# One transfer of q in five parts, with a matrix in its transposes that restores the order

## The chip, the cores and the metric

The kernel runs on one core of a Trainium2 chip. The metric is the device time of one execution in microseconds (us); smaller is better. The core has a matrix engine (TensorE, PE in the profile; its weight loads are PEld), VectorE (DVE), ScalarE (ACT), GpSimd (POOL) and SyncE (SP). Loads and stores are carried out by 16 DMA engines. POOL issues every load but one; SP issues that one and all stores.

## The reference

Two operators follow each other. The first is causal attention with a window of 64 positions, over 8 batches, 8 heads, 576 positions and a head dimension of 64:

```python
scores = scale * np.matmul(q, k.transpose(0, 1, 3, 2))
mask = (rel >= 0) & (rel < window)
scores = np.where(mask, scores, -1000000000.0)
attn = exp(scores - max); attn = attn / sum(attn)
return np.matmul(attn, v)
```

The second takes the result as x of shape 8 x 576 x 512, transforms it along the positions, multiplies the 64 lowest frequencies by one complex 512 x 512 matrix each (`w_r`, `w_i`), transforms back to y, forms u = x + y and returns u + max(u @ w_ch, 0). The 127 matrices that are needed (the imaginary one of frequency 0 has no effect) are 512 x 512 float32, 1 MiB each, and are by far the largest part of what is read from memory.

## The kernel before, in words

**Loads.** POOL issues a load for each of q, k and v of a batch (`load`, L109 to L112) and for each weight matrix (`load_w`, L138, one matrix; `load_two`, L144, two). The memory holds float32, the tiles in SBUF are bfloat16, and the transfer converts. A batch of q, 8 heads by 576 positions by 64, goes into a tile `rq` of 128 partitions x 2 x 1152: a partition's row in each of the two halves is a run of 18 positions of one head, 1152 elements, 4608 bytes in memory and 2304 in the tile. Half 0 holds heads 0 to 3 and half 1 heads 4 to 7, 32 partitions a head, in the order of the positions. A weight matrix goes into 128 partitions of 2048 elements. All loads go into one queue and are worked off in order.

**Order of the issues.** The first batches are loaded at the start. From then on `refill` (L402 to L414), called after each unit of transposes, loads batch b + 2 when a unit of batch b has freed its buffer, and one weight matrix behind it. The load of the last batch's q (b + 2 = 7) is issued after the q transposes of batch 5. Each issue on POOL waits in program order, for its buffer to be free and for the transfer that stands eight places before it to have landed, since the framework hands out eight completion semaphores in turn.

**Attention.** `transpose_units` (L234) gives 12 units a batch. Three `part`s each for k, v and q transpose 6 runs of 64 columns in two halves: the data tile is loaded as weights, and the identity `ident_bf` (128 x 128) is streamed through it, so that PSUM receives the transposed block; `evac` then copies it to `kT`, `vT` or `qT` with the columns in the order of positions. The column order that PSUM receives follows the matrix that is streamed. Scores, exponentials and the weighted sums follow in windows of 512 columns (`scores`, L305; `weigh`, L332), the transform of a finished batch in `dft` (L361).

**Weights.** From about 141 us on, `half(i)` (L610) multiplies matrix i: 16 matmuls per matrix, in the order of `order`, which is the order of the loads. When a matrix has been used, `issue` (L567) loads the next one into its place. Between the matrices PE does the second product, the inverse transform (L748 to L843), and, where there is nothing else, filler matmuls (`idle`, L901).

**End.** The last matrix is used by `half(T_I + 1)` (L1006). Behind it stand the last products, the rectification and the stores (L1008 to L1055), which can't start before it.

The order on PE and POOL is that of the program inside `manual_schedule`; on DVE and ACT the framework orders instructions in the main loop.

Of the kernel before, what the change touches and what calls it, by code (L numbers as in the profile page):

```python
# [11 lines left out]
BF16 = mybir.dt.bfloat16  # L12
# [8 lines left out]
def view(ap, off, dims):  # L21

    return bass.AP(ap.tensor, ap.offset + off, [list(ap.ap[0])] + [list(d) for d in dims])
# [3 lines left out]
def kernel(  # L27
# [10 lines left out]
    nc = tc.nc  # L38
    B, H, S, D = q.shape
# [8 lines left out]
    RUN = S // 32  # L48
# [6 lines left out]
    def evac(o, i, on_act):  # L55

        if on_act:
            return nc.scalar.copy(out=o, in_=i)  # L58
        return nc.vector.tensor_copy(out=o, in_=i)  # L59
# [10 lines left out]
    ident_bf = consts.tile([128, 128], BF16, name="ident_bf")  # L70
# [19 lines left out]
    acons = p1.enter_context(tc.tile_pool(name="acons", bufs=1, side="right"))  # L90
# [10 lines left out]
    RAW = {"k": k, "q": q, "v": v}  # L101

    def raw_tile(which):
        return rawp.tile([128, 2, RUN * D], BF16, name="r" + which)

    def runs(b, which):
        return RAW[which][b].rearrange("(x g) (p c) d -> (g p) x (c d)", g=4, c=RUN)

    def load(b, which):  # L109
        r = raw_tile(which)  # L110
        nc.gpsimd.dma_start(out=r, in_=runs(b, which))
        raws[b, which] = r  # L112


# [63 lines left out]
    with tc.manual_schedule(engines=ALL_FOUR):  # L178
# [3 lines left out]
        with tc.tile_pool(name="tmpf", bufs=1, side="right") as tmp:  # L182
            mo = tmp.tile([128, NM], FP32, name="mo")
            to = tmp.tile([128, NT], FP32, name="to")
            nc.gpsimd.iota(mo, pattern=[[1, NM]], base=0, channel_multiplier=0,
                           allow_small_or_imprecise_dtypes=True)
            nc.gpsimd.iota(to, pattern=[[128, NT]], base=0, channel_multiplier=1,
                           allow_small_or_imprecise_dtypes=True)
            nc.gpsimd.memset(ident, 0.0)
            nc.gpsimd.affine_select(out=ident, in_=ident, compare_op=ALU.not_equal, fill=1.0,  # L190
                                    base=0, pattern=[[-1, 128]], channel_multiplier=1)
            load(0, "q")
            load(0, "v")
            for t0, t1 in ((0, 3), (3, NT)):
                n = t1 - t0
                mt = tmp.tile([128, 2, n * NM], FP32, name="mtf")
                nc.vector.tensor_tensor(out=view(mt, 0, [[NM, n], [1, NM]]), in0=view(mo, 0, [[0, n], [1, NM]]),
                                        in1=view(to, t0, [[1, n], [0, NM]]), op=ALU.mult)
                gen_trig(tmp, mt, n * NM, trigF[:, t0:t1, 0:NM], trigF[:, t0:t1, NM:2 * NM], "f")
                if t0 == 0:  # L200
                    nc.vector.tensor_copy(out=ident_bf, in_=ident)
        nc.scalar.activation(out=spark, in_=ident[:, 0:1], func=ACT_F.Exp)
        raws[0, "k"] = raw_tile("k")
        for c, engine in enumerate((nc.vector, nc.gpsimd, nc.vector)):
            cc = slice(6 * D * c, 6 * D * (c + 1))
            engine.tensor_copy(out=raws[0, "k"][:, :, cc], in_=k_first[:, :, cc])
        load(1, "k")
        for i in range(4):
            half = i % 2
# [24 lines left out]
    def transpose_units(b):  # L234

        rk, rq, rv = (raws.pop((b, which)) for which in "kqv")
        qT = qtp.tile([128, 4, S], BF16, name="qT")
        vT = vtp.tile([128, 4, S], BF16, name="vT")
        kT, vt = kTs[b % 2], vts[b % 2]
        qTs[b] = qT  # L240

        def part(src, dst, c0, on_act):
            def f():
                ps = ps_misc.tile([128, 6, 128], BF16, name="pst", tag="misc")
                for c in range(6):
                    for hh in range(2):
                        nc.tensor.transpose(out=ps[64 * hh:64 * hh + 64, c, :],  # L247
                                            in_=src[:, hh, (c0 + c) * D:(c0 + c + 1) * D],
                                            identity=ident_bf)
                evac(view(dst, c0, [[S, 4], [RUN, 32], [1, 6]]),  # L250
                     view(ps, 0, [[32, 4], [1, 32], [128, 6]]), on_act)
            return f

        def vback(u):
            def f():
                ps = ps_misc.tile([128, 6, 128], BF16, name="psv", tag="misc")
                for i in range(6):
                    a, j = divmod(6 * u + i, 9)
                    if j == 4:
                        parts = [(0, 64, 2 * a, 512), (64, 64, 2 * a + 1, 0)]  # L260
                    else:
                        parts = [(0, 128, 2 * a + (j > 4), 128 * j - (j > 4) * S)]
                    for r0, n, g, t0 in parts:
                        nc.tensor.transpose(out=ps[r0:r0 + n, i, :],  # L264
                                            in_=vT[:, g, t0:t0 + n], identity=ident_bf)
                evac(view(vt, 6 * u * VW, [[18 * VW, 2], [VW, 6], [1, D]]),
                     view(ps, 0, [[D, 2], [128, 6], [1, D]]), u != 1)
                if u:
                    hs = slice(u - 1, u + 2, 2)
                    nc.vector.tensor_copy(out=vt[64:128, 1, hs, 1:9], in_=vt[64:128, 0, hs, 0:8])  # L270
                    nc.vector.tensor_copy(out=vt[0:64, 1, hs], in_=vt[0:64, 0, hs])
            return f

        return [part(rk, kT, 0, True), part(rk, kT, 6, False), part(rk, kT, 12, True),
                part(rv, vT, 0, False), part(rv, vT, 6, True), part(rv, vT, 12, False),
                part(rq, qT, 0, True), part(rq, qT, 6, False), part(rq, qT, 12, True),
                vback(0), vback(1), vback(2)]

    def head_of(n):
# [143 lines left out]
    with tc.manual_schedule(engines=ALL_FOUR):  # L423
        first = transpose_units(0)
        for j in (0, 1, 2, 6, 7, 8):
            first[j]()
            refill(0, j)
            if j in (2, 8):
                warm_up(3)
        for half in range(2):  # L430
            pp = slice(64 * half, 64 * half + 64)
            nc.vector.tensor_copy(out=band2[pp], in_=band[pp, half, :])
        mask(0, 1)
        scores(0)
        for j in (3, 4, 5):
            first[j]()
            refill(0, j)
            warm_up(2)
        for vt in vts:
            nc.vector.memset(vt[:, 0, :, :, 64:66], 1.0)  # L440
        for j in (9, 10, 11):
            first[j]()
            refill(0, j)
        nc.vector.memset(pso, 1.0)
        nc.vector.tensor_copy(out=ident_r, in_=ident)
    with tc.manual_schedule(engines={E.PE, E.Pool}):
# [9 lines left out]
        def unit(b, j):  # L456
            if b not in units:
                units[b] = transpose_units(b)
            units[b][j]()
            refill(b, j)  # L460
            turned(b, j)

        for w in range(NWIN + 1):
# [22 lines left out]
            if w in (NWIN - 4, NWIN - 1):  # L486
                i = (B - 2) % 2 if w == NWIN - 4 else (B - 1) % 2
                spare(kTs[i])
                spare(qtp.tile([128, 4, S], BF16, name="qT"))
            if w in (NWIN - 4, NWIN):  # L490
                i = (B - 2) % 2 if w == NWIN - 4 else (B - 1) % 2
# [386 lines left out]
    for k, (f, delta, n, few) in enumerate(items):  # L878
        i = S_I + k * (T_I - 2 - S_I) // len(items)
# [25 lines left out]
    with tc.manual_schedule(engines=ALL_FOUR):  # L905
# [92 lines left out]
        for k in range(6):  # L998
# [10 lines left out]
                              in_=view(psys[0], 0, [[2 * B, NC], [2, B], [1, 2]]))  # L1009
# [78 lines left out]
```

## Time and profile before

| | us |
|---|---|
| median of three runs | 425.67 (425.48 to 425.93) |
| the profiled execution, its own time | 425.65 |
| its span, first to last instruction | 423.8 |
| PE busy | 352.3 |
| DVE, ACT, POOL busy | 189.2, 159.8, 81.6 |

The span of the profile is 1.85 us shorter than that execution's own time. In the profile's views a time is in us from the start of the span. In the view of windows, each engine has its busy time and the number of its instructions in the stretch, and the last two columns are the mean busy share of the 16 DMA engines and the GB/s that arrive (bytes in SBUF's types, half of what is read). The packets of one DMA engine overlap a little in the records, so a fully used set of 16 shows 1.04 to 1.10. In the timeline, what stands in brackets is the time that the engine stood idle before the row, and what ended it.

### The profile page before, as it was taken

The numbers are of one execution on the slowest core, as the hardware profiler recorded it, in microseconds if no ns is written. First come the engines' busy times: TensorE is split into PE (matmuls) and PEld (weight loads), VectorE is DVE, ScalarE is ACT, GpSimd is POOL, SyncE is SP. The second block draws the span as 40 slices with busy tenths as digits, with TensorE's granted clock in tenths as the row PEclk, the third lists the DMA queues.
The fourth block names the chain that finished last, engine by engine and source line by source line (L and its number), as shares of the span: only waits on it lengthen the run. The fifth ranks groups of instructions, "written<-read, shape, count | busy, mean of one in ns | idle before, by whom it ended". The sixth has DMA issues, their size and how long they took to land.

```text
span 423.8 us, 11438 instructions
## 1 busy us (share of the span) xinstructions
PE 352.3 (83%) x5156; PEld 233.6 (55%) x5185; DVE 189.2 (45%) x359; ACT 159.8 (38%) x267; POOL 81.6 (19%) x146
## 2 busy tenths in 40 slices
PE   7799999999997779866669587767789899998994
PEld 3466656656654567644446455545556565554451
DVE  6676775766764001634332351121104345340895
ACT  5565766767754100122102110110023343330863
POOL 6322222221031130411112012120121112200000
PEclk9999999999999555966756656666579999999997
DMA  8999999999999999999999999999999999995598
GB/s 212 211 214 212 214 212 212 213 213 213 214 214 214 213 215 261 215 214 214 215 214 213 215 213 215 215 213 215 213 215 214 214 213 211 214 214 106 203 370 320
DMA packets 29920, 92.55 MB, mean 218 GB/s; under 512 B 2352, under 2 KB 2352, under 8 KB 29872
## 3 DMA queue, kind: packets, MB, share of 16 engines
q0 software_dynamic: 24624, 81.21, 95.9%
q1 hardware_dynamic: 5248, 10.62, 6.8%
q8 instruction: 40, 0.66, 0.6%
q14 instruction: 8, 0.07, 0.0%
HBM read 162.53 MB, written 9.44 MB: 406 GB/s over the span
## 4 chain that ended last, share of the span: by engine, by line
PE 42%; DMA 39%; DVE 7%; issue 5%; ACT 3%; POOL 0%; DVEq 0%; POOLq 0%; ACTq 0%
DMA wms<-in_moe_w_r_dram 20%; DMA wms<-in_moe_w_i_dram 19%; PE psy L618 7%; PE pso L343 6%; PE pst L247 5%; PE psv L264 3%; PE psx L365 3%; PE pss L963 3%; DVE x_sb L351 2%; PE pss L956 2%; PE pss L300 2%; PE pss L319 2%; PE psy L903 2%; DVE vT L59 2%; PE psf L800 1%
## 5 line engine op out<-in xcount | busy, mean ns | idle before, releaser
L759 PE MATMUL psz<-wch,xT 128*128 128x512 f32 x144 | 65.0, 594 | 0.0
L753 DVE CAST xT<-pxt 128x1024 fp32r<-128x1024 bf16 x18 | 22.0, 1224 | 78.0 <-PE pxt L748 78.0
L762 ACT CAST Z<-psz 128x1024 fp32r<-128x1024 f32 x18 | 18.2, 1012 | 102.2 <-PE psz L759 94.5
L325 ACT ACTIVATE et<-pss 128x512 bf16<-128x512 f32 x72 | 39.2, 599 | 13.7 <-PE pss L319 13.7
L618 PE MATMUL psy<-XQ,wls 128*128 128x16 bf16 x560 | 22.0, 192 | 23.7 <-DMA wls<-in_moe_w_r_dram 14.2
L759 PEld LDWEIGHTS psz<-wch,xT 128*128 128x128 f32 x144 | 37.4, 287 | 5.9
L618 PE MATMUL psy<-XQ,wms 128*128 128x16 bf16 x624 | 25.1, 192 | 17.9 <-DMA wms<-in_moe_w_i_dram 12.7
L618 PEld LDWEIGHTS <-wls 128*128 128x128 bf16 x560 | 19.5, 106 | 33.8 <-DMA wls<-in_moe_w_r_dram 17.4
L618 PEld LDWEIGHTS <-wms 128*128 128x128 bf16 x624 | 21.4, 103 | 30.2 <-DMA wms<-in_moe_w_i_dram 15.3
L343 PE MATMUL pso<-vt,et 128*64 128x65 bf16 (+1 forms) x576 | 32.3, 203 | 3.5 <-DVE x_sb L351 1.6
L811 DVE TENSOR_TENSOR Z<-pse,Z 128x1024 fp32r<-128x1024 f32 x16 | 19.6, 1225 | 29.3 <-PE pse L800 29.3
L343 PEld LDWEIGHTS <-et 128*64 128x64 bf16 (+1 forms) x576 | 22.2, 109 | 14.2 <-issue 6.7
L351 DVE TENSOR_TENSOR x_sb<-pso,rcp 128x640 bf16<-128x640 f32 x32 | 26.3, 822 | 0.9
L618 PE MATMUL psy<-XQ,wt 128*128 128x16 bf16 x560 | 20.5, 192 | 4.8 <-DMA wt<-in_moe_w_i_dram 2.3
L618 PEld LDWEIGHTS <-wt 128*128 128x128 bf16 x560 | 18.3, 104 | 11.2 <-DMA wt<-in_moe_w_i_dram 4.3
L59 DVE CAST YT<-psy 128x256 fp32r<-128x256 f32 x6 | 2.5, 424 | 42.0 <-PE psy L618 32.7
L59 DVE COPY vT<-pst 128x768 bf16<-128x768 bf16 x16 | 15.3, 958 | 12.9 <-PE pst L247 11.3
L981 ACT ACTIVATE pss<-pss 128x512 f32<-128x512 f32 x35 | 18.5, 581 | 4.7 <-PE pss L963 4.1
L300 PE MATMUL pss<-band,ident_bf 64*64 64x512 bf16 x120 | 16.5, 396 | 0.0
L264 PE MATMUL psv<-ident_bf,vT 128*128 128x128 bf16 (+1 forms) x160 | 15.6, 226 | 0.6 <-DVE vT L59 0.6
L58 ACT COPY vt<-psv 128x768 bf16<-128x768 bf16 x16 | 12.9, 807 | 8.3 <-PE psv L264 8.2
L58 ACT COPY qT<-pst 128x768 bf16<-128x768 bf16 x16 | 12.9, 813 | 6.4 <-PE pst L247 6.4
(191 smaller groups left out, 605.7 us busy)
## 6 DMA issues: line engine op xcount, KB each, us to landing
wt<-in_moe_w_i_dram POOLq DMA_DIRECT2D x19, 512.0 KB, 20.4
wt<-in_moe_w_r_dram POOLq DMA_DIRECT2D x16, 512.0 KB, 19.4
wls<-in_moe_w_r_dram POOLq DMA_DIRECT2D x8, 1024.0 KB, 21.8
wms<-in_moe_w_i_dram POOLq DMA_DIRECT2D x7, 1024.0 KB, 22.2
wms<-in_moe_w_r_dram POOLq DMA_DIRECT2D x7, 1024.0 KB, 21.6
wls<-in_moe_w_i_dram POOLq DMA_DIRECT2D x6, 1024.0 KB, 21.3
rq<-in_q_dram POOLq DMA_DIRECT2D x8, 576.0 KB, 15.3
rv<-in_v_dram POOLq DMA_DIRECT2D x8, 576.0 KB, 13.8
```

What stands on the lines that cost most here:

```text
L58: return nc.scalar.copy(out=o, in_=i)
L59: return nc.vector.tensor_copy(out=o, in_=i)
L247: nc.tensor.transpose(out=ps[64 * hh:64 * hh + 64, c, :], in_=src[:, hh, (c0 + c) * D:(c0 + c + 1) * D], identity=ident_bf)
L264: nc.tensor.transpose(out=ps[r0:r0 + n, i, :], in_=vT[:, g, t0:t0 + n], identity=ident_bf)
L300: nc.tensor.matmul(out=pss[(2 * w + hh) % 3][64 * half:64 * half + 64, :], lhsT=ident_bf[pp, pp], rhs=view(band[pp], 128 * half, [[0, WIN ...
L325: nc.scalar.activation(out=et[:, hh, :], in_=pss[(2 * w + hh) % 3], func=ACT_F.Exp, scale=EX_SCALE)
L343: nc.tensor.matmul(out=pso[po, hh, block(b, i // 2) * VW:block(b, i // 2) * VW + D + 1], lhsT=et[pk, hh, col:col + 64], rhs=vt[pk, 1 - f % ...
L351: nc.vector.tensor_tensor(out=view(x_sb, b * NT * DM + g * D, [[4 * D, 2], [DM, NT], [1, D]]), in0=view(pso, 0, [[512, 2], [VW, NT], [1, D]]),
L618: nc.tensor.matmul(out=view(psy, off + 2 * B * e, [[1, 2 * B]]), lhsT=w[:, c, 128 * e:128 * e + 128], rhs=XQ[:, m // HM, c, :, 1 - im:3 - ...
L753: nc.vector.tensor_copy(out=o, in_=i)
L759: nc.tensor.matmul(out=psz[s][:, j, :], lhsT=xts[s % 2][0][:, j, 128 * c:128 * c + 128], rhs=wch[:, c, :], start=(c == 0), stop=(c == NC - 1))
L811: nc.vector.tensor_tensor(out=z, in0=ps, in1=z, op=ALU.add)
```

## The change

For the last batch's q alone, the one load becomes three, and a fourth small one follows. Half 0 of the tile, 128 rows, is split: the first 125 rows are moved by one transfer whose source is written as five parts of 25 rows, where part a takes rows a, a + 5, a + 10 and so on; it fills partitions 0 to 124. Half 1 (128 rows) and the last 3 rows of half 0 are moved by plain transfers. The small one moves 16 elements of each of 22 rows, in 11 parts of 2, to a tile `aside` that nothing reads. Partition 25a + r of half 0 then holds row 5r + a. To undo this, a matrix `back` is made on DVE: a copy of the identity in which the first 125 columns are permuted. The transposes of half 0 of this q stream `back` and not `ident_bf`; their number and shapes stay.

```diff
+    UNEVEN = (B - 1, "q")
+    FEW, MORE = 5, 25
+    LOT = FEW * MORE
+    aside = acons.tile([2 * (16 - FEW), 16], BF16, name="aside")
+    back = acons.tile([128, 128], BF16, name="back")
+
     def load(b, which):
         r = raw_tile(which)
-        nc.gpsimd.dma_start(out=r, in_=runs(b, which))
+        if (b, which) == UNEVEN:
+            lower, upper = [RAW[which][b, x * H // 2:(x + 1) * H // 2].rearrange("g (p c) d -> (g p) (c d)", c=RUN)
+                            for x in range(2)]
+            nc.gpsimd.dma_start(out=r[:LOT, 0, :], in_=lower[:LOT].rearrange("(r a) c -> a r c", a=FEW))
+            nc.gpsimd.dma_start(out=r[:, 1, :], in_=upper)
+            nc.gpsimd.dma_start(out=r[LOT:, 0, :], in_=lower[LOT:])
+            nc.gpsimd.dma_start(out=aside, in_=lower[:2 * (16 - FEW), 0:16].rearrange("(r a) c -> a r c", a=16 - FEW))
+        else:
+            nc.gpsimd.dma_start(out=r, in_=runs(b, which))
         raws[b, which] = r
...
-        def part(src, dst, c0, on_act):
+        def part(src, dst, c0, on_act, uneven=False):
             def f():
                 ps = ps_misc.tile([128, 6, 128], BF16, name="pst", tag="misc")
+                if uneven and c0 == 0:
+                    nc.vector.tensor_copy(out=back, in_=ident_bf)
+                    nc.vector.tensor_copy(out=view(back, 0, [[1, FEW], [FEW, MORE]]),
+                                          in_=view(ident_bf, 0, [[MORE, FEW], [1, MORE]]))
                 for c in range(6):
                     for hh in range(2):
                         nc.tensor.transpose(out=ps[64 * hh:64 * hh + 64, c, :],
                                             in_=src[:, hh, (c0 + c) * D:(c0 + c + 1) * D],
-                                            identity=ident_bf)
+                                            identity=back if uneven and hh == 0 else ident_bf)
...
-                part(rq, qT, 0, True), part(rq, qT, 6, False), part(rq, qT, 12, True),
+                *(part(rq, qT, 6 * i, i != 1, (b, "q") == UNEVEN) for i in range(3)),
```

In the built program the instructions of PE, ACT and SP stand in the same order as before. The two copies that make `back` do not stand where the last q is transposed, but at the start of DVE's program, behind the first cast to `ident_bf` and ahead of the second half of the cosine table (L167). POOL's program has three transfers more.

## The prediction

> **What bounds the kernel now.** I first read the chain of work that ended last, from the page and then in order of time.
>
> ```profile
> span 423.8 us, 11438 instructions
> ...
> PE 42%; DMA 39%; DVE 7%; issue 5%; ACT 3%; POOL 0%; DVEq 0%; POOLq 0%; ACTq 0%
> ```
>
> ```profile
> 361.37 13.62 DMA wms<-in_moe_w_r_dram
> 375.06 0.90 issue
> 375.98 14.40 DMA wms<-in_moe_w_i_dram
> 390.43 0.65 PE psy L618 x16
> ```
>
> The last weight matrix is issued at 375.98, lands 14.40 us later at about 390.4, and PE uses it at 390.43. Behind it stand 33.4 us of products and stores (423.8 - 390.43), which the change doesn't touch. So the question is when the load stream ends. Next I read how busy the 16 DMA engines are in the last stretch (view of windows; the last but one column is their share).
>
> ```profile
> 380.00:384.40 4.40, 4.00 (x46) 2.25 (x46) 0.84 (x2) 0.58 (x1) 0.00 (x0) 1.00 1.04 209
> 384.40:385.60 1.20, 0.74 (x5) 0.13 (x4) 0.00 (x0) 0.00 (x0) 0.00 (x0) 1.00 0.58 116
> 385.60:386.60 1.00, 1.00 (x18) 0.94 (x19) 0.32 (x1) 0.00 (x0) 0.00 (x0) 1.00 0.51 102
> 386.60:387.60 1.00, 0.88 (x4) 0.38 (x2) 0.07 (x1) 0.35 (x1) 0.00 (x0) 1.00 0.55 111
> 387.60:389.00 1.40, 0.98 (x19) 0.74 (x20) 0.00 (x0) 0.00 (x0) 0.00 (x0) 1.00 0.51 102
> 389.00:389.80 0.80, 0.80 (x6) 0.33 (x4) 0.00 (x0) 0.00 (x0) 0.00 (x0) 1.00 0.14 26
> 389.80:390.50 0.70, 0.44 (x5) 0.07 (x3) 0.00 (x0) 0.00 (x0) 0.00 (x0) 1.00 0.00 0
> ```
>
> A full set shows 1.04. From 385.60 to 389.00 it is 0.51 to 0.55: half of the engines, eight of sixteen, are still moving data, the other eight have nothing left. Most of the early eight end near 384.4, since the share is already 0.58 from there to 385.60. The late eight end between 389.0 and 389.8, and one a little later, since the last landing is at about 390.4. So the stream is not at its end because all engines are full, but because half of them are some 4.6 us behind. Had the work that stands in these rows been dealt evenly, it would take (1.20 x 0.58 + 1.00 x 0.51 + 1.00 x 0.55 + 1.40 x 0.51 + 0.80 x 0.14) / 1.06 = 2.4 us from 384.4 and end at 386.8: 3.6 us is the most that any dealing of loads can bring.
>
> The page of the DMA queues up to 391 us shows one kind of traffic that is not dealt evenly by the program.
>
> ```profile
> q0 software_dynamic: 24624, 81.21, 104.0%
> ...
> q8 instruction: 39, 0.64, 0.6%
> q14 instruction: 7, 0.06, 0.0%
> ```
>
> Instruction packets (q8) take 0.6% of 16 engines over 391 us, 37.5 us in all; on eight engines that would be 4.7 us each, about the lag. That these are the cause is not shown, and no view says which engines are late; the lag itself is what counts here.
>
> **The change, part by part.** *Rows taken from the engines.* The price of one row comes from a stretch in which only q, k and v arrive.
>
> ```profile
> DMA packets 1934, 4.24 MB, mean 212 GB/s; under 512 B 112, under 2 KB 112, under 8 KB 1931
> ...
> q0 software_dynamic: 1931, 4.19, 110.2%
> ```
>
> A row is 2304 bytes in the tile; 16 engines at 212 GB/s take 2304 x 16 / 212 = 174 ns a row and engine. Before, each engine moves 8 of the 128 rows of half 0 (and 8 of half 1, which stay). I read the five parts as five engines with 25 rows each. Then five engines have 17 rows more, 17 x 0.174 = 2.96 us, and eleven have 8 less, 8 x 0.174 = 1.39 us. If the five are early ones, they end near 384.4 to 385.6 + 2.96 = 387.4 to 388.6, the eight late ones end 1.39 us sooner, and the last landing is at 390.4 - 1.39 = 389.0. This is the main term, -1.39 us.
>
> [...]
>
> *The 3 rows, `aside` and three more completions.* The 3 rows cost the engines that get them 0 to 0.17 us (one row each); I take 0.05, since three of sixteen get one and only the last engine counts. `aside` gives 11 engines two pieces of 64 bytes; two full rows, 0.35 us, bound it above and nothing below; I take 0.10, nearer to nothing because the bytes are few. Three more transfers mean three more completion packets an engine (the 112 under 512 B above are of this kind); no row prices one, between nothing and a row each, 0 to 0.52 us; I take 0.05, since one stands behind every load and the rate above holds with them inside. None of the three can be a gain.
>
> *POOL's queue.* Three more issues, at 0.5 to 0.7 us each as below, and more important, each takes a place in the eight.
>
> ```profile
> 87.78 0.70 POOL L111 DMA_DIRECT2D rq<-in_q_dram  x1 [2.23 <-PE pst L247]
> 88.84 0.56 POOL L138 DMA_DIRECT2D wt<-in_moe_w_i_dram  x1 [0.36 <-DMA wt<-in_moe_w_i_dram]
> 91.28 0.54 POOL L138 DMA_DIRECT2D wt<-in_moe_w_r_dram  x1 [1.88 <-DMA rq<-in_q_dram]
> 93.74 0.53 POOL L138 DMA_DIRECT2D wt<-in_moe_w_r_dram  x1 [1.92 <-DMA wt<-in_moe_w_r_dram]
> 96.58 0.53 POOL L138 DMA_DIRECT2D wt<-in_moe_w_i_dram  x1 [2.31 <-DMA rk<-in_k_dram]
> ```
>
> The load of 87.78 alone, from issue to landing:
>
> ```profile
> DMA to landing us min/median/max: 19.0/19.0/19.0
> ```
>
> After the change the transfers at 88.84, 91.28 and 93.74 are the two plain ones and `aside`, and the weight load of 88.84 moves to 96.58, 7.7 us later; the next three and those of line 138 into the freed tiles shift by as many places. The order in the DMA queue stays, so this costs nothing while the engines have work. Cover: q is issued 19.0 us before it lands; with half 1, the 3 rows and `aside` holding three of eight places, five full loads of about 2.5 us (the spacing of the rows above) remain, some 10 to 12 us. If the cover went, an idle stretch would add itself to the end one to one. I take 0.
>
> *When q is there.* It lands at 87.78 + 19.0 = 106.8, by the reading above 3 us later at most on five engines, 109.8. It is first used here:
>
> ```profile
> 115.94 0.53 PE L247 MATMUL pst<-ident_bf,rq 128*64 128x128 bf16 x12
> ```
>
> 6 us remain: 0. The transposes with `back` are as many and as large: 0.
>
> *The two copies on DVE.* They stand at the start of the program, ahead of the second half of the cosine table.
>
> ```profile
> 3.14 0.22 DVE L201 CAST ident_bf<-ident 128x128 bf16<-128x128 f32 x1
> ...
> 5.99 1.65 DVE L206 CAST rk<-x_sb 128x768 bf16<-128x768 f32 x2 [0.93 <-DMA x_sb<-in_k_dram]
> ```
>
> ```profile
> L659 DVE COPY turns_bf<-ident_bf 128x128 bf16<-128x128 bf16 x1 | 0.7, 670 | 0.0
> ```
>
> The plain one costs some 0.22 us, the strided one at most 0.67, as the copy of L659: 0.9 us, beside 0.93 us in which DVE waits for k. ACT's table part (L171, L172) and its first copies move by as much at worst; PE is then up to 0.9 us late at the start. That is hidden later, where PE waits for loads:
>
> ```profile
> 316.50 0.66 PE L618 MATMUL psy<-XQ,wls 128*128 128x16 bf16 x16 [1.20 <-DMA wls<-in_moe_w_r_dram]
> ...
> 331.44 0.64 PE L618 MATMUL psy<-XQ,wms 128*128 128x16 bf16 x16 [0.95 <-DMA wms<-in_moe_w_i_dram]
> ...
> 383.19 0.65 PE L618 MATMUL psy<-XQ,wt 128*128 128x16 bf16 x16 [0.35 <-DMA wt<-in_moe_w_r_dram]
> ...
> 385.59 0.65 PE L618 MATMUL psy<-XQ,wt 128*128 128x16 bf16 x16 [0.46 <-DMA wt<-in_moe_w_i_dram]
> ...
> 388.02 0.64 PE L618 MATMUL psy<-XQ,wt 128*128 128x16 bf16 x16 [0.54 <-DMA wt<-in_moe_w_r_dram]
> ...
> 390.43 0.65 PE L618 MATMUL psy<-XQ,wms 128*128 128x16 bf16 x16 [0.26 <-DMA wms<-in_moe_w_i_dram]
> ```
>
> These rows also tell whether PE can follow an earlier stream. It is ready only 0.26 to 0.54 us before each of the last four matrices, less than the 1.39 us; between 331.44 and 365 it waits for no load at all. But that work starts at the landing for which it waited 1.20 us at 316.50 and 0.95 us at 331.44. A landing 1.2 us earlier lets PE start 1.2 us earlier at 316.50 and carries that on to the end. So I take the whole gain.
>
> *Sum.* -1.39 + 0.05 + 0.10 + 0.05 = -1.19 us. Against the profiled execution's own 425.65 us: 424.46, say 424.5 (0.28% less). The median of the runs, 425.67, is 0.02 us from that execution. With the bounds: -1.39 gives 424.3; all three small costs at their upper ends, -1.39 + 0.17 + 0.35 + 0.52 = -0.35, give 425.3.
>
> **The rivals.** *The five engines are late ones, or some are* (the other side). Nothing in the profile says which engines are late, and eight of sixteen are. One late engine among the five decides it: with 25 rows for 8 it ends 2.96 us later, from 389.8 to 392.8, or, if it is the very last, from 390.4 to 393.4, and everything behind follows. 425.65 + 2.4 to 3.0, with 0 to 0.2 for the small transfers: 428.0 to 428.8, say 428.3. It also covers the case that the place of the five changes from one execution to the next, since most places then have a late one among them. For it: the even split of early and late. Against it: if the late ones lie in one block, a run of five fits beside it, and the excess of 2.96 us is within the lag of 4.6.
>
> *PE takes over the bound.* If its work from 331.44 on did not move with the stream, the last landing could gain no more than the 0.26 us that PE waits for it: 425.4. Against it stand the 1.20 and 0.95 us above.
>
> *The transfer is dealt to all sixteen as the others are.* Then each engine moves about 8 rows as before, and only the small costs are left, at my values +0.2: 425.9, or 425.7 at none. For it: every load in this trace keeps the full share of 1.04 to 1.10 on all engines, so far as the view shows.
>
> **How the numbers follow.** Forecast 0.52, late engines 0.32, sixteen engines 0.10, PE 0.06. The predicted time is that of the likeliest, 424.5, with its own range of 424.2 to 425.3. Forecast, sixteen engines and PE hold 0.68; for 0.8 the range must take in most of the late case: 424.1 to 428.7. A measurement of this kernel can tell about 0.2%, 0.85 us. Of the forecast, 0.46 is faster by more than that and 0.06 is not (small costs near their ends); the two middle rivals with that make 0.22 for no change; slower 0.32.
>
> **What would show it.** Right: the first of the four transfers lands on time, the last matrix is used near 389.2, and the stretch with a share near 0.5 is about 1.4 us shorter, with more than half of the engines busy until about 387.5. Late engines: the last matrix is used near 393, and the last 3 us show a share of 0.3 or less, five engines or fewer. Sixteen: the end as in the windows above. PE: rows of L618 after 380 without a wait for DMA. The sum fails if the queue runs dry near 100 us, seen as a share well below 1.04 there.

## The result, and the profile after

The changed kernel takes 424.29 us (median, 424.13 to 424.43), the kernel before beside it 425.63 us (425.39 to 426.01). The ratio is 0.9968, with an interval of 0.9958 to 0.9978: 0.32% faster, where 0.28% was forecast. The profiled execution of the changed kernel took 424.43 us, with a span of 422.7 us. In its trace the line numbers are higher by the lines that were added: L618 became L638, L138 became L154, L111 became L122 to L125.

The end of the chain of work that ended last, of the kernel after (start, length, what):

```profile
374.20 0.90 issue
...
375.12 14.08 DMA wms<-in_moe_w_i_dram
389.20 0.05 issue
389.25 0.65 PE psy L638 x16
```

The last weight matrix lands at 389.20; before, it landed at 375.98 + 14.40 = 390.38. That is 1.18 us sooner. What stands behind it is as long as it was: 422.7 - 389.25 = 33.45 us against 33.37. The whole gain is thus in the load stream. Its last stretch in the view of windows, kernel after (last but one column: share of the 16 DMA engines):

```profile
379.00:383.20 4.20, 3.82 (x46) 2.11 (x45) 1.01 (x2) 0.59 (x1) 0.00 (x0) 1.00 1.04 210
383.20:384.40 1.20, 1.20 (x10) 0.46 (x9) 0.00 (x0) 0.00 (x0) 0.00 (x0) 1.00 0.90 181
384.40:385.40 1.00, 1.00 (x19) 0.91 (x18) 0.39 (x1) 0.00 (x1) 0.00 (x0) 1.00 0.84 168
385.40:386.40 1.00, 0.78 (x4) 0.30 (x2) 0.00 (x0) 0.35 (x1) 0.00 (x0) 1.00 0.82 164
386.40:387.80 1.40, 1.06 (x19) 0.78 (x20) 0.00 (x0) 0.00 (x0) 0.00 (x0) 1.00 0.79 158
387.80:388.60 0.80, 0.80 (x6) 0.29 (x3) 0.00 (x0) 0.00 (x0) 0.00 (x0) 1.00 0.29 56
388.60:389.40 0.80, 0.45 (x7) 0.16 (x6) 0.00 (x0) 0.00 (x0) 0.00 (x0) 1.00 0.00 0
```

Sixteen engines show about 1.06, so one shows 0.066. Where 0.51 to 0.55 stood before (eight engines), 0.79 to 0.84 stands now: 12 to 13 engines, the eight late ones and five more. Only three end before 384.4. By 388.6 nearly all have ended. So the five engines that were given more rows were early ones.

The issues on POOL, kernel after (start, length, engine, line, what; in brackets the idle time before and what ended it):

```profile
88.97 0.70 POOL L122 DMA_DIRECT2D rq<-in_q_dram  x1 [2.24 <-PE pst L267]
89.68 0.57 POOL L123 DMA_DIRECT2D rq<-in_q_dram  x1
91.42 0.73 POOL L124 DMA_DIRECT2D rq<-in_q_dram  x1 [1.17 <-DMA rq<-in_q_dram]
93.89 0.56 POOL L125 DMA_DIRECT2D aside<-in_q_dram  x1 [1.73 <-DMA wt<-in_moe_w_r_dram]
96.92 0.55 POOL L154 DMA_DIRECT2D wt<-in_moe_w_i_dram  x1 [2.47 <-DMA rk<-in_k_dram]
```

The weight load that stood at 88.84 now stands at 96.92. The engines were never without work meanwhile, as two windows of the kernel after show (share 1.09, where 1.07 stands before for the second):

```profile
88.00:100.00 12.00, 11.46 (x231) 7.25 (x226) 7.74 (x15) 7.47 (x15) 3.66 (x6) 1.00 1.09 212
100.00:112.00 12.00, 11.85 (x275) 8.24 (x273) 8.98 (x18) 9.28 (x18) 2.65 (x5) 1.00 1.09 211
```

The start of DVE's program, kernel after:

```profile
3.32 0.20 DVE L262 COPY back<-ident_bf 128x128 bf16<-128x128 bf16 x1
3.55 0.51 DVE L263 COPY back<-ident_bf 128x125 bf16<-128x125 bf16 x1
...
6.02 1.65 DVE L222 CAST rk<-x_sb 128x768 bf16<-128x768 f32 x2 [1.05 <-DMA x_sb<-in_k_dram]
```

The two copies take 0.71 us, and the first cast of k starts at 6.02 against 5.99, still waiting for its transfer. They cost nothing.

The last matrices that PE waits for, kernel after:

```profile
382.45 0.65 PE L638 MATMUL psy<-XQ,wt 128*128 128x16 bf16 x16 [0.38 <-DMA wt<-in_moe_w_r_dram]
...
386.74 0.65 PE L638 MATMUL psy<-XQ,wt 128*128 128x16 bf16 x16 [0.56 <-DMA wt<-in_moe_w_r_dram]
...
389.25 0.65 PE L638 MATMUL psy<-XQ,wms 128*128 128x16 bf16 x16 [0.35 <-DMA wms<-in_moe_w_i_dram]
```

Of the last four matrices PE waits 0.35 to 0.56 us for these three; the one between the first two, at 384.28, was there when PE came to it. PE has followed the earlier stream, and loads remain the bound.

### The profile page after: what moved, and what is told of

It reads as the page before. It is cut to its first block, busy times and chain, and to the rows that moved or that the text cites. A ratio compares the mean times of both kernels' runs of the same rounds, so it can differ in the third digit from the quotient of the medians.

```text
span 422.7 us, 11472 instructions
## 1 busy us (share of the span) xinstructions
PE 352.8 (83%) x5185; PEld 232.3 (55%) x5185; DVE 189.0 (45%) x361; ACT 159.9 (38%) x267; POOL 83.7 (20%) x149
## 4 chain that ended last, share of the span: by engine, by line
DMA 45%; PE 39%; DVE 7%; issue 2%; ACT 2%; DVEq 0%; POOLq 0%; ACTq 0%
DMA wms<-in_moe_w_i_dram 23%; DMA wms<-in_moe_w_r_dram 22%; PE psy L638 6%; PE pso L363 6%; PE pst L267 5%; PE psv L284 3%; PE psx L385 3%; PE pss L983 3%; DVE x_sb L371 2%; PE pss L976 2%; PE pss L320 2%; PE pss L339 2%; PE psz L779 2%; DVE vT L59 2%; PE psy L923 2%
## 5 line engine op out<-in xcount | busy, mean ns | idle before, releaser
L779 PE MATMUL psz<-wch,xT 128*128 128x512 f32 x144 | 61.2, 564 | 0.0
L638 PE MATMUL psy<-XQ,wms 128*128 128x16 bf16 x624 | 25.0, 192 | 20.1 <-DMA wms<-in_moe_w_i_dram 12.3
L638 PE MATMUL psy<-XQ,wls 128*128 128x16 bf16 x560 | 21.9, 192 | 23.2 <-DMA wls<-in_moe_w_r_dram 14.4
L638 PEld LDWEIGHTS <-wms 128*128 128x128 bf16 x624 | 21.3, 102 | 32.3 <-DMA wms<-in_moe_w_i_dram 15.5
L779 PEld LDWEIGHTS psz<-wch,xT 128*128 128x128 f32 x144 | 34.9, 268 | 5.4
L638 PEld LDWEIGHTS <-wls 128*128 128x128 bf16 x560 | 19.6, 105 | 32.6 <-DMA wls<-in_moe_w_r_dram 17.2
L638 PEld LDWEIGHTS <-wt 128*128 128x128 bf16 x560 | 18.4, 105 | 11.1 <-issue 4.2
L638 PE MATMUL psy<-XQ,wt 128*128 128x16 bf16 x560 | 20.5, 192 | 4.4 <-DMA wt<-in_moe_w_i_dram 1.7
L923 PE MATMUL psy<-trigF,ident_bf 128*128 128x512 bf16 x46 | 18.4, 465 | 0.1
```

Source lines behind the costliest of these rows:

```text
L638: nc.tensor.matmul(out=view(psy, off + 2 * B * e, [[1, 2 * B]]), lhsT=w[:, c, 128 * e:128 * e + 128], rhs=XQ[:, m // HM, c, :, 1 - im:3 - ...
L779: nc.tensor.matmul(out=psz[s][:, j, :], lhsT=xts[s % 2][0][:, j, 128 * c:128 * c + 128], rhs=wch[:, c, :], start=(c == 0), stop=(c == NC - 1))
L923: nc.tensor.matmul(out=o, lhsT=ident_bf, rhs=view(trigF, 0, [[1, DM]]), start=True, stop=True)
```

## The experiments

The prediction gave no reason why the five engines should be early ones. It only said that a run of five fits beside the late ones if these lie in one block. The theory to test was therefore: *place decides; the five parts go to five consecutive engines, the transfer is the first of its kind, and the late engines form a block elsewhere.* That the five are neighbours, and that each part moves the place on by one engine, was assumed; the trace records no engine's number. The rivals were that the late ones are scattered, and that the engines don't matter at all. In each experiment below the diff is against the changed kernel. All of them compute the whole reference.

**Another place: three, four or eleven engines further.** A small transfer of 3, 4 or 11 parts goes ahead of the five parts and by the theory moves the place; the one behind has 8 or 7 parts, or falls away. Shown for 3; the other two differ in these numbers only:

```diff
+    ahead = acons.tile([6, 16], BF16, name="ahead")
-    aside = acons.tile([2 * (16 - FEW), 16], BF16, name="aside")
+    aside = acons.tile([16, 16], BF16, name="aside")
...
+            nc.gpsimd.dma_start(out=ahead, in_=lower[:6, 0:16].rearrange("(r a) c -> a r c", a=3))
             nc.gpsimd.dma_start(out=r[:LOT, 0, :], in_=lower[:LOT].rearrange("(r a) c -> a r c", a=FEW))
...
-            nc.gpsimd.dma_start(out=aside, in_=lower[:2 * (16 - FEW), 0:16].rearrange("(r a) c -> a r c", a=16 - FEW))
+            nc.gpsimd.dma_start(out=aside, in_=lower[:16, 0:16].rearrange("(r a) c -> a r c", a=8))
```

> Theory (place): the gain comes from which five engines take the 25 rows; in the changed kernel these are five neighbours that finish early, and a transfer in n parts moves the place on by n. Here three parts of the aside transfer go first, so the five move on by three engines; the sum of 16 and the output stay. If the early eight are one block that begins where the five began, the five still lie in it: 424.3 us, 0.3% below before. Rival (scattered): early and late engines alternate or lie in smaller groups; then a late one is among them and the time is 428.0 to 428.8. Rival (no place): the gain comes from the split of the load or the later issues, not from engines; 424.3 here and in every other shift.

> The same with four parts first and seven last. Theory (place), early block of eight that begins where the five began: the fifth of the five is now the first late engine, with 17 rows more; end of the stream 2.4 to 3.0 us later than before, 428.0 to 428.8 us, and at the end one engine alone (a share of about 0.07) is busy. If the block reaches further or begins earlier: 424.3. Rival (no place): 424.3.

> All eleven parts of the aside transfer first, then the five: they lie on the five engines before the place at which they began. Theory (place), early block of eight that begins at the old place: all five are late ones, 428.0 to 428.8 us, and at the end five engines (a share of about 0.33) are busy for some 3 us. Rival (no place): 424.3, with four transfers and the same order of issues.

Measured: 427.98 us for three (ratio 1.0062, 1.0047 to 1.0077), 427.92 for four (1.0054, 1.0039 to 1.0069), 428.84 for eleven (1.0073, 1.0056 to 1.0090), against 425.68 before. All three are slower than the kernel before, and 3.6 to 4.6 us slower than the changed kernel, with the same work in the same program but for an almost empty transfer. The last us in windows, shift by three:

```profile
389.00:390.00 1.00, 0.69 (x3) 0.22 (x2) 0.00 (x0) 0.26 (x1) 0.00 (x0) 1.00 0.12 25
390.00:391.00 1.00, 0.76 (x18) 0.64 (x19) 0.00 (x0) 0.00 (x0) 0.00 (x0) 1.00 0.12 25
391.00:392.00 1.00, 1.00 (x6) 0.43 (x5) 0.00 (x0) 0.00 (x0) 0.00 (x0) 1.00 0.16 33
```

Shift by four:

```profile
390.00:391.00 1.00, 0.85 (x18) 0.68 (x19) 0.00 (x0) 0.00 (x0) 0.00 (x0) 1.00 0.14 29
```

Shift by eleven:

```profile
390.00:391.00 1.00, 1.00 (x5) 0.52 (x3) 0.23 (x1) 0.35 (x1) 0.00 (x0) 1.00 0.28 57
391.00:392.00 1.00, 0.45 (x15) 0.41 (x15) 0.00 (x0) 0.00 (x0) 0.00 (x0) 1.00 0.27 53
392.00:393.00 1.00, 1.00 (x14) 0.52 (x10) 0.00 (x0) 0.00 (x0) 0.00 (x0) 1.00 0.26 53
```

At 0.066 an engine, two engines are last with three and with four (0.12 to 0.16), where one was expected with four, and four with eleven (0.26 to 0.28), where five were expected. So place decides, and the rival that it does not is out. But the theory's other half fell as well: the late engines are not one block, for each of these places holds some, and not the same number.

**Eight parts, from the same place.** Half 0 in eight parts of 16 rows and the small one in eight: eight engines have 16 rows for 8, and the three rows apart fall away.

```diff
-    FEW, MORE = 5, 25
+    FEW, MORE = 8, 16
...
-            nc.gpsimd.dma_start(out=r[:LOT, 0, :], in_=lower[:LOT].rearrange("(r a) c -> a r c", a=FEW))
+            nc.gpsimd.dma_start(out=r[:, 0, :], in_=lower.rearrange("(r a) c -> a r c", a=FEW))
             nc.gpsimd.dma_start(out=r[:, 1, :], in_=upper)
-            nc.gpsimd.dma_start(out=r[LOT:, 0, :], in_=lower[LOT:])
-            nc.gpsimd.dma_start(out=aside, in_=lower[:2 * (16 - FEW), 0:16].rearrange("(r a) c -> a r c", a=16 - FEW))
+            nc.gpsimd.dma_start(out=aside, in_=lower[:16, 0:16].rearrange("(r a) c -> a r c", a=8))
```

> Half 0 of the last q in eight parts of 16 rows, no transfer of three rows, eight aside parts. Theory (place) with an early block of eight: late engines lose 8 rows, 1.39 us, as with five parts; early ones gain 8, 1.39 us, and end near 386 to 387; last landing near 389.1, 424.2 us. If the block has fewer than eight from the old place on: one late engine gets 8 rows more, 427.0 us. Rival (no place): 424.3 as well, but then the shares at the end would show eight engines busy to the last as before.

Measured: 426.50 us, ratio 1.0020 (1.0010 to 1.0029). Windows of this kernel:

```profile
389.00:390.00 1.00, 1.00 (x18) 0.63 (x15) 0.00 (x0) 0.00 (x0) 0.00 (x0) 1.00 0.14 29
```

The time is 0.5 us under the 427.0 that was expected with a late engine among the eight. The share of 0.14 is two engines: two late ones are among the eight. Together the four kernels and the changed one give a map, if the engines are counted from the first of the five, taken in order, and the start is the same in each kernel: none late in 0 to 4 (the changed kernel), two in 5 to 7 (eight parts), two in 3 to 7 (agrees), two in 4 to 8 (so 8 is early), four in 11 to 15. Eight are late in all, so 9 and 10 are late too. A run of five without a late engine then starts at 0, or at most also at 1 and at 15: one to three of sixteen places. The four kernels ran together on one chip, and the changed kernel was not run beside them there; the map supposes that its place and its late engines are the same. For it speaks that kernels with the five parts at the same place took 424.59 and 424.37 us on two other chips (the four further transfers and the kernel without `aside`, both below).

**Both halves uneven.** The same five engines get 25 rows of half 1 too.

```diff
-    aside = acons.tile([2 * (16 - FEW), 16], BF16, name="aside")
+    aside = [acons.tile([2 * (16 - FEW), 16], BF16, name=f"aside{x}") for x in range(2)]
...
-            nc.gpsimd.dma_start(out=r[:LOT, 0, :], in_=lower[:LOT].rearrange("(r a) c -> a r c", a=FEW))
-            nc.gpsimd.dma_start(out=r[:, 1, :], in_=upper)
-            nc.gpsimd.dma_start(out=r[LOT:, 0, :], in_=lower[LOT:])
-            nc.gpsimd.dma_start(out=aside, in_=lower[:2 * (16 - FEW), 0:16].rearrange("(r a) c -> a r c", a=16 - FEW))
+            for x, half in enumerate((lower, upper)):
+                nc.gpsimd.dma_start(out=r[:LOT, x, :], in_=half[:LOT].rearrange("(r a) c -> a r c", a=FEW))
+                nc.gpsimd.dma_start(out=r[LOT:, x, :], in_=half[LOT:])
+                nc.gpsimd.dma_start(out=aside[x], in_=half[:2 * (16 - FEW), 0:16].rearrange("(r a) c -> a r c", a=16 - FEW))
...
-                                            identity=back if uneven and hh == 0 else ident_bf)
+                                            identity=back if uneven else ident_bf)
```

> Both halves of the last q in five parts (two transfers of 125 rows, two of 3, two aside transfers). Theory (place, 174 ns a row): the eleven others lose 16 rows, 2.8 us, but the five gain 34 rows, 5.9 us, more than their lead of 4.6 us: they become the last, from 384.4 to 385.6 + 5.9 = 390.3 to 391.5 against a last landing of 390.4 before; 425.7 to 426.8 us, and at the end five engines are busy (share 0.33). Rival (what counts is only what the late ones lose): 390.4 - 2.8 = 387.6, 422.9 us.

Measured: 427.13 us, ratio 1.0032 (1.0020 to 1.0044), 0.3 us above the expected band. Windows of this kernel:

```profile
389.00:390.00 1.00, 0.74 (x18) 0.62 (x19) 0.00 (x0) 0.00 (x0) 0.00 (x0) 1.00 0.39 78
390.00:391.00 1.00, 1.00 (x6) 0.45 (x5) 0.00 (x0) 0.00 (x0) 0.00 (x0) 1.00 0.16 33
```

From 389 to 390 the share of 0.39 is six engines, five of them presumably those with 34 rows more: 34 x 0.174 = 5.9 us, more than the lag of 4.6. That both halves went to the same five can be read from the trace itself, which keeps each packet with its size (no view lists them): a row of q is a packet of 2304 bytes, and from 102 to 110 us close to five such packets are under way at any time, never eight. The excess has a limit, and twice the change is past it.

**Between the two.** In each half, 95 rows in five parts of 19 and 33 rows in eleven parts of 3, with nothing aside: five engines have 22 rows more in all, eleven have 10 fewer.

```diff
-            nc.gpsimd.dma_start(out=r[:LOT, 0, :], in_=lower[:LOT].rearrange("(r a) c -> a r c", a=FEW))
-            nc.gpsimd.dma_start(out=r[:, 1, :], in_=upper)
-            nc.gpsimd.dma_start(out=r[LOT:, 0, :], in_=lower[LOT:])
-            nc.gpsimd.dma_start(out=aside, in_=lower[:2 * (16 - FEW), 0:16].rearrange("(r a) c -> a r c", a=16 - FEW))
+            for x in range(2):
+                half = RAW[which][b, x * H // 2:(x + 1) * H // 2].rearrange("g (p c) d -> (g p) (c d)", c=RUN)
+                nc.gpsimd.dma_start(out=r[:95, x, :], in_=half[:95].rearrange("(r a) c -> a r c", a=5))
+                nc.gpsimd.dma_start(out=r[95:, x, :], in_=half[95:].rearrange("(r a) c -> a r c", a=11))
...
-                    nc.vector.tensor_copy(out=back, in_=ident_bf)
-                    nc.vector.tensor_copy(out=view(back, 0, [[1, FEW], [FEW, MORE]]),
-                                          in_=view(ident_bf, 0, [[MORE, FEW], [1, MORE]]))
+                    for o, k, n in ((0, 5, 19), (95, 11, 3)):
+                        nc.vector.tensor_copy(out=view(back, o, [[1, k], [k, n]]),
+                                              in_=view(ident_bf, o, [[n, k], [1, n]]))
...
-                                            identity=back if uneven and hh == 0 else ident_bf)
+                                            identity=back if uneven else ident_bf)
```

> Each half of the last q by two transfers, 95 rows in five parts and 33 in eleven parts, so that no aside transfer and no transfer of 3 rows is needed and the place is back after each half. The five gain 2 x 11 = 22 rows, 3.8 us, and end at 388.2 to 389.4; the eleven lose 2 x 5 = 10 rows, 1.7 us, last landing 390.4 - 1.7 = 388.7. Theory (place): the end lies between these, 388.7 to 389.4, so 423.9 to 424.6 us, at or a little below the changed kernel. Rival (PE can't follow more than it does): 424.3, with rows of the weight products that wait for no load after 380.

Measured: 425.02 us, ratio 0.9980 (0.9971 to 0.9989). It is faster than the kernel before, and 0.7 us slower than the changed one: a miss by 0.4 us. Chain and windows of this kernel:

```profile
376.03 13.76 DMA wms<-in_moe_w_i_dram
389.79 0.05 issue
```

```profile
388.00:389.00 1.00, 1.00 (x7) 0.45 (x5) 0.00 (x0) 0.00 (x0) 0.00 (x0) 1.00 0.19 37
389.00:390.00 1.00, 0.69 (x9) 0.20 (x8) 0.00 (x0) 0.00 (x0) 0.00 (x0) 1.00 0.02 4
```

From 388 to 389 the share of 0.19 is three engines' worth, and what is left after 389.0 is less than one engine's worth of a us; the landing is at 389.79. Whether that last one is among the five or one of the eleven was not found.

**What an almost empty transfer costs.** Four further transfers of 16 pieces of 64 bytes, one behind the k load of batches 3 to 6, are added to the changed kernel; nothing reads them.

```diff
+    tiny = acons.tile([16, 4, 16], BF16, name="tiny")
...
+        if which == "k" and 3 <= b < 7:
+            nc.gpsimd.dma_start(out=tiny[:, b - 3, :], in_=RAW["k"][b, 0, 0:16, 0:16])
```

> The changed kernel with four more transfers of 16 pieces of 64 bytes to a tile that nothing reads, one behind each k load of batches 3 to 6. What one almost empty transfer costs the stream. By the prediction's terms (0.05 us for three completions, 0.10 us for the aside pieces) four cost under 0.5 us: 424.3 to 424.8. If such a transfer takes an engine as long as a full row of 174 ns or more whatever it moves: 4 x 0.17 to 0.2 = 0.7 to 0.8 us, 425.0 to 425.1 us.

Measured: 424.59 us, ratio 0.9974 (0.9964 to 0.9983). That is 0.30 us over the changed kernel's 424.29, which was not run beside it, and the intervals of the two ratios overlap: some 0.08 us a transfer, not told from nothing, and by the medians less than the 0.174 us of a full row.

**The 125 rows without the parts.** The first transfer moves the same 125 rows in their own order, and all transposes stream the identity. The split, the 3 rows and the small transfer stay.

```diff
-            nc.gpsimd.dma_start(out=r[:LOT, 0, :], in_=lower[:LOT].rearrange("(r a) c -> a r c", a=FEW))
+            nc.gpsimd.dma_start(out=r[:LOT, 0, :], in_=lower[:LOT])
...
-                                            identity=back if uneven and hh == 0 else ident_bf)
+                                            identity=ident_bf)
```

> The first transfer moves the same 125 rows in their own order, not in five parts, and all transposes stream the plain identity; the other three transfers stay. Theory (parts make it): a plain transfer of 125 partitions is dealt to all engines, 8 rows each, as the full loads are; the gain is gone and the three small costs are left, 425.7 to 426.0 us, with a stretch near 0.5 at the end. Rival (125 alone does it, since five divides it): 424.3 us, as the changed kernel, and the parts and the restoring matrix are not needed.

Measured: 425.78 us, ratio 0.9985 (0.9963 to 1.0008), not told apart from the kernel before. Windows of this kernel:

```profile
385.60:389.00 3.40, 2.67 (x31) 1.61 (x30) 0.39 (x1) 0.35 (x1) 0.00 (x0) 1.00 0.54 107
```

The share is 0.54, eight engines, as before the change. So a plain transfer of 125 partitions is dealt evenly enough to leave the lag as it was, and the five parts are what moves the rows.

**Without `aside`.** If the position were kept from one execution to the next, the small transfer of eleven parts would be needed to bring it round.

```diff
-    aside = acons.tile([2 * (16 - FEW), 16], BF16, name="aside")
...
-            nc.gpsimd.dma_start(out=aside, in_=lower[:2 * (16 - FEW), 0:16].rearrange("(r a) c -> a r c", a=16 - FEW))
```

> The changed kernel without the aside transfer. Theory (the place is kept from one execution to the next and moves on by the number of parts): the five begin five engines further in each execution, so the place walks through all sixteen; by the runs with the aside moved, most places hold a late engine. The runs of this kernel then differ among themselves by some 4 us, from 424.2 to about 429, most of them above before; a single profile can show either. Rival (every execution begins at the same place): all runs agree within 0.5 us at 424.2, and the aside transfer is not needed.

Measured: 424.37 us, ratio 0.9971 (0.9961 to 0.9982), its eight runs from 424.14 to 424.68. Windows of this kernel:

```profile
384.40:387.80 3.40, 2.88 (x35) 1.84 (x32) 0.39 (x1) 0.35 (x1) 0.00 (x0) 1.00 0.80 160
```

No run shows the 3.6 to 4.6 us that a bad place costs, and 0.80 is again twelve to thirteen engines. The theory that the place wanders fell: in these runs each begins at the same place, and `aside` isn't needed. What sets the place back was not found; where executions are chained in another way, it may matter. No version was clearly faster than the changed kernel; this one equals it with a transfer less.

## Why the prediction was right, point by point

- **Rows taken from the late engines, -1.39 us.** Held. The last landing is 1.18 us sooner; forecast with the small costs was 1.19. It can't be carried further as it stands: with ten rows fewer on eleven engines (1.74 us) and 22 more on five, the landing moved by 0.6 us only (390.38 to 389.79), and why was not found. That the rows must go to few engines is shown by the 125 plain rows, which bring nothing. The five engines were to end at 387.4 to 388.6; the share falls from 0.79 to 0.29 at 387.8.
- **That the five engines are early ones.** Right in the outcome, but not for its reason. "A run of five fits beside it" supposed one block of late engines, and the shifts by three, four and eleven show them scattered. By the map, one to three of sixteen places are good. That the five parts fell on one of them was luck, and 0.52 for the forecast was too sure: no view of the profile of before told the place. The rival's price was close: 428.3 by its text, 427.92 to 428.84 in the three shifted kernels. Of its bounds for the last landing, 392.8 to 393.4, the shifts by three and four fell just short (392.65 and 392.56), and the shift by eleven, with four late engines, came 0.7 us past them (394.06). There the stream ran dry for a while: POOL's issues follow the late engines (the one of 336.61 in the kernel before stands at 340.03), and from 345 to 350 us the share is 0.85, where it is 1.05 before. Over these 5 us about 1 us of full work is missing.
- **What decides the engines.** That five parts go to five engines was a reading of the edit; the trace of the kernel after bears it out. It has sixteen completion records for each load, though no view lists them: for the weight matrix that lands at 104.34, ahead of this q, none is more than 2.65 us behind the first, and for the one that lands at 110.70, behind it, five are 4.36 to 5.00 us behind and the others at most 2.69; 25 rows are 25 x 0.174 = 4.35 us. The same 125 rows without the parts leave the share at 0.54. That the engines are neighbours, from a place that the parts issued ahead move on, no trace shows; the times agree with it (424.29 at 0; 427.98, 427.92 and 428.84 at 3, 4 and 11). That the sizes 5 and 11 add up to 16 is not what kept the place: without the eleven parts the runs lie from 424.14 to 424.68 all the same. With the transfer of 3 rows the sum would be 5 + 3 + 11 = 19. That this one doesn't move the place is shown by the kernel with both halves uneven: there it stands, with the eleven parts, between the two fives, and by the packets both went to the same five engines.
- **Dealt to all sixteen.** Wrong for the five parts, right for the same rows without them: 425.78, where 425.7 to 425.9 had been worked out.
- **PE takes over the bound.** Wrong: PE uses the last matrix at 389.25, 1.18 us sooner than before, and waits 0.35 us for it, 0.26 before. One row after 380, at 384.28, stands without a wait, which was to be this rival's sign, but the later ones wait again, and the gain came.
- **The small costs, 0.20 us.** They fit in sum, -1.39 + 0.20 = -1.19 against -1.18, but were not resolved one by one. Four more small transfers cost some 0.30 us together, against which 0.05 for three completions and 0.10 for `aside` are of a fitting size; taking `aside` away changed the median by 0.08 us, less than the runs scatter. No run shows on how many engines the pieces of `aside` lie. And the three transfers bring more small packets than three completions an engine: up to 391 us the kernel after has 2352 packets under 512 B and the one before 1984, 368 more, of which 22 are the pieces of `aside` and 48 would be three completions on sixteen engines; what the other 298 are was not found.
- **POOL's queue, 0.** Held: the load moved to 96.92 (96.58 was worked out), and the share stays at 1.09 from 88 to 112 us.
- **When q is there, 0.** Held. By the view of that line the five parts were 17.7 us from issue to landing, so they landed at 88.97 + 17.7 = 106.7; the slowest part of q, the 3 rows, landed at 91.42 + 16.8 = 108.2, under the bound of 109.8.
- **The copies on DVE, 0.** Held: 0.71 us of 0.9, and DVE still waits 1.05 us for k behind them.

Why half of the engines are late was left open by the prediction. The trace of the kernel before bears on it with two kinds of records that no view lists: the length of each packet, and the sixteen completion records of each load. The lengths of the 39 instruction packets repeat, but for a few longer ones, with a period of eight (893, 893, 949, 945, 935, 974, 974 and 961 ns, then again from 893), as if eight engines took turns. Of a load's sixteen completions, the last eight are on average 1.7 us behind the first eight for the matrix that lands at 103.94, after 14 such packets; 3.2 us for the one at 187.24, after 25; and 4.8 us for the last one, after 39: each time 0.12 to 0.13 us a packet, about 1 us for one of eight engines. At 103.94 two of the last eight are only some 1.2 us behind the early ones, and with the next two instruction packets, at 106.12 and 112.18, just these two fall back by about 1 us each. From these times it is inferred that the late eight are the engines that also carry the instruction packets; no run changed the number of instructions to test it.

Still open are two things. What sets the place back. And the three engines that are neither late nor among the five: they end before 384.4, some 4 us ahead of the rest; these 12 engine-us dealt over sixteen would be some 0.8 us more.

## What to carry to other kernels

Where a stream of loads sets the end, look at the share of the DMA engines in its last few us before counting its bytes: here 0.51 to 0.55 meant that eight engines were done and the other eight decided (by its completion records the last matrix was complete on eight from 384.52 to 385.53 and on eight from 389.16 to 390.39), and rows taken from all of the late ones brought about their time (1.18 us of 1.39). Here a source written in five parts put the rows on five engines (424.29 us, where the same 125 rows without the parts took 425.78), but which engines these are is not in any view; try several places on the chip, since here the same edit changed the time by -0.32% at one place and +0.54 to +0.73% at three others. Keep the excess under the lag, with room: 17 rows (2.96 us) gained 1.34 us, 34 rows (5.9 us) lost 1.40 us.

## What the runs showed of the hardware

- The late engines are scattered: counted from the first of the five, by the map above, none in 0 to 4, two in 5 to 7, 9 and 10, four in 11 to 15. The map rests on the assumption that the engines are taken in order; that eight are late is shown without it (share 0.51 to 0.55; completions of the last matrix 4.8 us behind those of the other eight). In the trace of before the lag grows with the instruction packets, 1.7 us after 14, 3.2 after 25 and 4.8 after 39; most of these packets are 892 to 975 ns long, and two of the engines fell back by about 1 us at one packet each.
- The place at which a transfer of five parts begins is the same in each execution here, by the times of the kernel without `aside` (424.14 to 424.68). A place that each part moves on by one engine, and that is kept from one execution to the next, would have wandered there.
- A few engines that end late hold back the others: in the shift by eleven, four engines with 17 rows more put the last landing at 394.06, 0.7 us past the bound worked out from their rows alone. The issues follow the late ones, and between 345 and 350 us some engines were without work (share 0.85 against 1.05), about 1 us of full work.
- An almost empty transfer in a full stream costs some 0.08 us, not told from nothing, though it takes a place among the eight that POOL has under way here: the issue at 96.58 of the kernel before waits for the k load issued at 80.42, eight places ahead.
